# Attention maxima over every fourth query, with one transfer for each shift row

## The chip, the cores and the metric

The kernel runs on one core of a Trainium2 chip. The metric is the device time of one execution in microseconds (us). A core has TensorE (PE in the profile, with its weight loads listed apart as PEld), VectorE (DVE), ScalarE (ACT), GpSimd (POOL) and SyncE (SP), whose queue issues most of the transfers.

## The reference

A transformer block for one sequence of 2048 tokens with 512 channels: a modulated layer norm, attention with 32 heads of 16 channels, a second modulated layer norm, a token mixer with shifts, and an MLP with 1792 hidden channels. What matters here is the attention:

```python
qkv = (x @ wqkv).reshape(B, S, 3, H, Dh).transpose(2, 0, 3, 1, 4)
q, k, v = qkv[0], qkv[1], qkv[2]
scores = jnp.einsum("bhqd,bhkd->bhqk", q, k) * (Dh ** -0.5)
p = _softmax(scores, axis=-1)
o = jnp.einsum("bhqk,bhkd->bhqd", p, v)
...
x = x + ga * _A_ref(h, A_wqkv, A_wo)
h = _layernorm(x, axis=-1) * (1 + cb) + sb
x = x + gb * _B_ref(h, B_w1, B_w2, B_w3, B_w4)
```

The softmax needs the largest score of each query before it takes exponentials, so that these stay in range.

## The kernel before

The work goes in three parts: the projections to queries, keys and values (with the layer norm), the attention, and the tail with the output projection, the mixer and the MLP. The first part runs on into the first quarter of the attention.

**Units.** The attention is cut into 64 units: four chunks of 512 queries (`ci`), and in each 16 pairs of heads (`pr`). The two heads of a pair, j = 0 and 1, lie on partitions 0 to 63 and 64 to 127 of the tiles `qtl` (queries, 512 columns) and `kst` (keys, 2048 columns), which exist three times each and are loaded by `load_unit`. A head takes 48 of its 64 partitions for a query or key in three parts (a high part twice and a low part, which together give more digits). Partitions 62 and 63 of a half are the shift rows: the key tile has ones there, so what stands in the query tile's rows 62 and 63 is added to every score of that query.

**Maxima first, scores later.** A unit's keys are passed over twice. `max_part` multiplies 128 queries (the weights of the product, taken from rows 0 to 61 of `qtl`) with 512 keys, and VectorE's `reduce_max` (line 989) reduces the product over its keys into one column of `mxs`. Four groups of queries (`g`), four stretches of keys (`c`) and two heads make 32 such products for each unit. In the code before, group `g` takes every second query of half `g // 2` of the chunk, starting at `g % 2` (line 986), so that its 128 words lie two words apart in a row of `qtl`.

When a unit's last maxima are there, `max_fin` reduces over the four stretches, turns the maxima into shifts, and splits them into two parts in `nm` (partition p, part i, column 4 j + g). `shift_rows` then writes them into the rows 62 and 63 of the query tile. Since a maximum stands on a partition and must go to a column, each transfer reads all 128 partitions and writes one row; before, there are two such transfers for a row (`h`), each over half of the 512 columns, with two neighbouring columns of `nm` for each partition. There are four rows (j and i), thus eight transfers for a unit, all on SP's queue. They are issued through `sch.dma`.

`score_part` later multiplies 128 keys with the 512 queries, shift rows included; ScalarE (line 1005) turns the product into exponentials written in a form whose high and low 16 bits are used apart. GpSimd or ScalarE makes the low part ready (`p_low`, line 1058), and `pv_part` multiplies both with the values (lines 1080 and 1083).

**Order of the work.** All orders are written out when the program is built. Time runs in steps `s`, one for each 128 keys of a unit, and half-steps for the two heads. Three half-steps make a block (`GRP`). `row_pair` puts a score product of one head and a maxima product of the other side by side, on the two halves of TensorE's rows. The maxima run 24 steps ahead of the scores (`LEAD`), so a unit's shift is asked for some nine steps before its first score. Products of both kinds take turns in seven PSUM banks (`NSM`). The planner `Sched` keeps an estimated clock for each engine and for SP's queue: `sch.dma` books

```python
self.T["S"] = max(self.T["S"], self.T["P"]) + max(n / DBW, 475.0)
```

for each transfer (in ns), and the times it returns decide where later stores, releases and pieces of the projections are put in the order.

Of the kernel before, what the change touches and what calls it, by code (L numbers as in the profile page):

```python
# [8 lines left out]
F32 = mybir.dt.float32  # L9
# [318 lines left out]
def kernel(ctx, tc, A_x, A_wqkv, A_wo, B_w1, B_w2, B_w3, B_w4, c, w_mod, out):  # L328
    nc = tc.nc
    te, act, dve, pool, dma = nc.tensor, nc.scalar, nc.vector, nc.gpsimd, nc.sync  # L330
# [21 lines left out]
    def mark(key):  # L352
        return None, 0, lambda: done.add(key)
# [64 lines left out]
    sch = Sched()  # L418
# [535 lines left out]
    qst, vst, mxs = {}, {}, {}  # L954
# [18 lines left out]
    def bank(nm):  # L973
        x = sm.take()
        return x, ap_.tile([P, CH], F32, name=nm, tag=f"s{x}", bufs=1)

    def max_part(m, j):

        u, i = divmod(m, 16)
        c, g = divmod(i, 4)  # L980
        if u not in mxs:
            mxs[u] = at.tile([P, 2, 4, NC], F32, name="mx", tag="mx", bufs=2)
        x, b = bank("mb")
        ready, sm.t[x] = sm.t[x], LATE
        r = slice(64 * j, 64 * j + 62)
        lhs = qst[u][r, (g // 2) * 256:(g // 2 + 1) * 256].rearrange("p (n l) -> p l n", l=2)[:, g % 2]

        def after(e):
            end = sch.crit("D", 605, e + PX, lambda: dve.reduce_max(mxs[u][:, j, g, c:c + 1], b, axis=AX.X))  # L989
            sm.t[x] = end + XP["D"]  # L990
            if (c, g, j) == (NC - 1, 3, 0):
                max_fin(u)
        return ready, lambda: te.matmul(b, lhs, kst[u % 3][r, c * CH:(c + 1) * CH], start=True, stop=True), after  # L993
# [17 lines left out]
    def row_pair(s, j):  # L1011

        parts = []
        if 0 <= s < NS:
            parts.append((j, score_part(s, j)))
        if s + LEAD < NS:
            parts.append((1 - j, max_part(s + LEAD, 1 - j)))
        parts = [x for _, x in sorted(parts, key=lambda x: x[0])]

        def mms():  # L1020
            for _, mm, _ in parts:
                mm()
        e = sch.put("P", CROW, max(x[0] for x in parts), mms)
        return [partial(x[2], e) for x in parts]

    def max_fin(u):
        mf = at.tile([P, 8], F32, name="mf", tag="mf", bufs=2)
        nm = at.tile([P, 2, 8], F32R, name="nm", tag="nm", bufs=2)
        mx = mxs.pop(u)

        def shift_rows():
            for j in range(2):
                for i in range(2):
                    r = 64 * j + 62 + i
                    for h in range(2):
                        sch.dma(dma.dma_start,
                                qst[u][r:r + 1, h * 256:(h + 1) * 256].bitcast(F32).rearrange("o (p l) -> o p l", l=2),
                                nm[:, i, 4 * j + 2 * h:4 * j + 2 * h + 2].bitcast(F32))
        sch.chain(("D", 85, lambda: dve.reduce_max(mf.rearrange("p (j g) -> p j g", j=2), mx, axis=AX.X)),
                  ("A", 100, lambda: act.activation(mf, mf, AF.Copy, scale=-1.0, bias=PEXP)),  # L1040
                  ("A", 100, lambda: act.activation(nm[:, 0], mf, AF.Copy)),
                  ("G", 250, lambda: pool.tensor_tensor(nm[:, 1], mf, nm[:, 0], op=OP.subtract)),
                  (None, 0, shift_rows), mark(("shift", u)), prio=0, ready=sch.T["D"])
# [554 lines left out]
    for k, blk in enumerate(blocks + [[]] * (LAG + CPER)):  # L1598
# [22 lines left out]
        n = 0  # L1621
# [105 lines left out]
```

## Time and profile before

| What | Value |
|---|---|
| Median of 3 runs | 2027.61 us (2023.54 to 2027.86) |
| Profiled execution, its own time | 2030.02 us |
| Its span, first to last instruction | 2028.2 us |
| Mean granted TensorE clock | 0.987 |
| Maxima products, and transfers of shift rows | 2048, and 512 |

Lines of the profile name a line of the code, an engine, an operation, and the tiles as output <- inputs: `mb` is a maxima product, `sc` a score product, `pt` the exponentials, `pv` the sum over values, `mx` the maxima, `nm` the shifts. In groups, the numbers behind the count are the busy time in us, the mean of one in ns, and the engine's idle time before them in us with what ended it. A matmul's record holds its passage through the array as well, so that several overlap; weight loads (PEld) run beside matmuls. `SPq` is SP's queue.

### The profile page before, as it was taken

To read this page: it belongs to the slowest core of one execution; us is meant where nothing else is said; L and a number is where in the kernel's file an instruction comes from. 1 tells how busy PE (TensorE), PEld (TensorE's weight loads), DVE (VectorE), ACT (ScalarE), POOL (GpSimd) and SP (SyncE) were. 2 spreads that over 40 slices of the span, in tenths; PEclk is the share of its full clock that TensorE was granted. 3 is DMA by queue.
4 is the path that set the end of the run, shared out by engine and by line. 5 is a ranking of instruction groups with operands and counts; after the bars stand their busy time and mean duration, and the time that the engine had idled before them with its cause. 6 is when DMAs were issued, how large, how long until landed. Compare 5 with 4: busy or idle time off the path is not lost.

```text
span 2028.2 us, 41674 instructions
## 1 busy us (share of the span) xinstructions
PE 1941.1 (96%) x14456; PEld 1168.8 (58%) x14456; DVE 1658.8 (82%) x2979; ACT 1511.4 (75%) x3085; POOL 1569.9 (77%) x1488
## 2 busy tenths in 40 slices
PE   8999999999999999999999999999998889999999
PEld 5755554554444444444444444444447778898998
DVE  6398788879999999999999999999965786556443
ACT  6438887768999989999999999999984554344443
POOL 6349998879999999999999999999994554335222
PEclk9989999999999999999999999999999899999999
DMA  8877666544443435353434343454414677553541
GB/s 302 233 203 183 158 190 165 135 126 118 81 97 81 97 72 106 72 107 72 107 72 98 80 102 76 95 162 93 90 38 146 228 261 274 218 201 122 200 154 68
DMA packets 185508, 278.01 MB, mean 137 GB/s; under 512 B 117104, under 2 KB 127856, under 8 KB 169008
## 3 DMA queue, kind: packets, MB, share of 16 engines
q1 hardware_dynamic: 181792, 267.20, 49.0%
q10 hardware_dynamic: 2304, 4.20, 0.6%
q0 software_dynamic: 1200, 3.93, 0.5%
q8 instruction: 115, 1.88, 0.4%
q14 instruction: 97, 0.79, 0.1%
HBM read 211.81 MB, written 62.91 MB: 135 GB/s over the span
## 4 chain that ended last, share of the span: by engine, by line
PE 61%; DVE 16%; ACT 10%; issue 6%; POOL 4%; DMA 3%; SPq 1%; ACTq 0%; POOLq 0%; DVEq 0%
PE mb L993 13%; DVE mx L989 11%; PE pv L1083 9%; PE sc L1009 8%; ACT pt L1005 7%; PE w L360 6%; PE w L356 6%; PE w L358 6%; PE pv L1080 4%; PE ot L1110 3%; POOL pt L1058 2%; PE xT L1244 1%; DMA wr<-Ws 1%; DMA wst<-in_A_wqkv_dram 1%; SPq L132 1%
## 5 line engine op out<-in xcount | busy, mean ns | idle before, releaser
L989 DVE TENSOR_REDUCE mx<-mb 128x1 f32<-128x512 f32 x2048 | 1250.1, 680 | 74.5 <-PE mb L993 68.6
L1058 POOL TENSOR_SCALAR pt<-pt 128x1024 f16<-128x1024 uint16 x953 | 1248.1, 1365 | 78.7 <-ACT pt L1005 75.7
L1005 ACT ACTIVATE pt<-sc 128x512 int32<-128x512 f32 x2048 | 1061.3, 615 | 125.6 <-PE mb L993 98.0
L993 PE MATMUL mb<-kst,qtl 62*128 62x512 f32 x2048 | 782.7, 462 | 19.9 <-ACT pt L1005 9.9
L1009 PE MATMUL sc<-qtl,kst 64*128 64x512 f32 x2048 | 739.7, 449 | 5.0 <-DVE mx L989 2.5
L993 PEld LDWEIGHTS mb<-kst,qtl 62*128 62x128 f32 x2048 | 360.1, 193 | 232.3 <-ACT pt L1005 159.9
L1009 PEld LDWEIGHTS sc<-qtl,kst 64*128 64x128 f32 x2048 | 337.0, 186 | 186.8 <-DVE mx L989 119.3
L1083 PE MATMUL pv<-pt,vst 128*32 128x512 f16 x4096 | 385.3, 397 | 20.5 <-ACT ac L1100 20.5
L1456 POOL TENSOR_TENSOR g<-sq,g 128x256 fp32r<-128x256 f32 (+1 forms) x124 | 97.2, 787 | 200.6 <-ACT g L1455 187.2
L1080 PE MATMUL pv<-pt,vst 128*32 128x512 f16 (+1 forms) x2048 | 220.8, 389 | 2.5 <-POOL pt L1058 2.4
L1083 PEld LDWEIGHTS <-vst 128*32 128x32 bf16 x4096 | 91.8, 93 | 227.7 <-issue 209.2
L358 PE MATMUL w<-A,wr 128*128 128x256 f32 (+1 forms) x520 | 156.1, 300 | 0.3 <-DVE A L346 0.3
L356 PE MATMUL w<-A,wr 128*128 128x256 f32 (+1 forms) x520 | 155.9, 300 | 0.2 <-ACT A L350 0.2
L360 PE MATMUL w<-A,wr 128*128 128x256 f32 (+1 forms) x520 | 155.8, 300 | 0.0
L1452 ACT ACTIVATE sq<-w 128x256 f32<-128x256 f32 (+1 forms) x130 | 52.3, 402 | 136.0 <-PE w L360 127.2
L356 PE MATMUL w<-wr,g 128*128 128x512 f32 x270 | 106.9, 396 | 2.9 <-DMA wr<-Ws 2.9
L360 PE MATMUL w<-wr,g 128*128 128x512 f32 x270 | 106.5, 394 | 0.9 <-POOL g L1456 0.9
L358 PE MATMUL w<-wr,g 128*128 128x512 f32 x270 | 106.1, 393 | 0.0
L1434 DVE SCALAR_TENSOR_TENSOR sq<-sq,w 128x256 f32<-128x256 f32 (+1 forms) x130 | 58.3, 449 | 57.7 <-ACT sq L1454 57.5
L356 PEld LDWEIGHTS w<-A,wr 128*128 128x128 f32 x520 | 101.7, 196 | 1.6 <-ACT A L350 0.5
L358 PEld LDWEIGHTS w<-A,wr 128*128 128x128 f32 x520 | 101.5, 195 | 1.5 <-DVE A L346 0.5
L360 PEld LDWEIGHTS w<-A,wr 128*128 128x128 f32 x520 | 101.3, 195 | 0.5 <-issue 0.5
(156 smaller groups left out, 2128.5 us busy)
## 6 DMA issues: line engine op xcount, KB each, us to landing
wr<-Ws SPq DMA_DIRECT2D x66, 1024.0 KB, 5.5
vst<-Vs SPq DMA_DIRECT2D x64, 768.0 KB, 5.6
kst<-Ks SPq DMA_DIRECT2D x126, 384.0 KB, 6.2
Ws<-wr SPq DMA_DIRECT2D x14, 1024.0 KB, 6.2
qtl<-Qs SPq DMA_DIRECT2D x128, 96.0 KB, 4.3
Vs<-vt SPq DMA_DIRECT2D x32, 384.0 KB, 4.2
Ks<-qk SPq DMA_DIRECT2D x16, 512.0 KB, 4.2
Qs<-qk SPq DMA_DIRECT2D x16, 512.0 KB, 3.0
```

What stands on the lines that cost most here:

```text
L356: te.matmul(o, lh, rh, start=first, stop=False)
L358: te.matmul(o, lh, rl, start=False, stop=False)
L360: te.matmul(o, ll, rh, start=False, stop=last)
L989: end = sch.crit("D", 605, e + PX, lambda: dve.reduce_max(mxs[u][:, j, g, c:c + 1], b, axis=AX.X))
L993: return ready, lambda: te.matmul(b, lhs, kst[u % 3][r, c * CH:(c + 1) * CH], start=True, stop=True), after
L1005: ea = sch.crit("A", 480, e + PX, lambda: act.activation(pt[s][:, j], b, AF.Exp))
L1009: return ready, lambda: te.matmul(b, kst[u % 3][r, kt * P:(kt + 1) * P], qst[u][r], start=True, stop=True), after
L1058: e_low[s] = XP["G"] + sch.crit("G", 1345, ready, lambda: pool.tensor_scalar(o, i, 0.5, 1.0, op0=OP.mult, op1=OP.mult))
L1080: te.matmul(acc[r:r + n, :], v[:, kt + i, c:c + n].bitcast(F16), pt[s + i].bitcast(F16)[:, j, 0::2], start=False, stop=kt == NKT - 2, skip ...
L1083: te.matmul(acc[r:r + 32, :], v[:, kt, r:r + 32], pt[s].bitcast(F16)[:, j, 1::2], start=kt == 0, stop=False, skip_group_check=True)
L1110: te.matmul(b[:, t * n:(t + 1) * n], ac[:, t * P:(t + 1) * P], smat.rearrange("p j d -> p (j d)"), start=True, stop=True)
L1456: ("G", cG(n), lambda: pool.tensor_tensor(lo, sq, hi, op=OP.subtract)), (None, 0, end), bank=b)
```

## The change

A group of a maxima product takes every fourth query of the whole chunk, starting at `g`, instead of every second of a half. With that the four maxima on a partition belong to four neighbouring queries, and a shift row is written by one transfer with four columns of `nm` instead of two transfers with two. The number of maxima products, of reductions and of all other instructions stays as it was; the transfers of shift rows go from eight to four for each unit.

```diff
@@ -983,7 +983,7 @@
         r = slice(64 * j, 64 * j + 62)
-        lhs = qst[u][r, (g // 2) * 256:(g // 2 + 1) * 256].rearrange("p (n l) -> p l n", l=2)[:, g % 2]
+        lhs = qst[u][r, :].rearrange("p (n l) -> p l n", l=4)[:, g]
...
@@ -1032,10 +1032,8 @@
                     r = 64 * j + 62 + i
-                    for h in range(2):
-                        sch.dma(dma.dma_start,
-                                qst[u][r:r + 1, h * 256:(h + 1) * 256].bitcast(F32).rearrange("o (p l) -> o p l", l=2),
-                                nm[:, i, 4 * j + 2 * h:4 * j + 2 * h + 2].bitcast(F32))
+                    sch.dma(dma.dma_start, qst[u][r:r + 1, :].bitcast(F32).rearrange("o (p l) -> o p l", l=4),
+                            nm[:, i, 4 * j:4 * j + 4].bitcast(F32))
```

## The prediction

> **What bounds the kernel now.** I read the time by engine first, then the windows by stage, the groups of instructions of the long stage, its waits, the chain of waits, and last the weight loads one by one.
>
> ```profile
> span 2028.2 us, 41674 instructions
> PE 1941.1 (96%) x14456; PEld 1168.8 (58%) x14456; DVE 1658.8 (82%) x2979; ACT 1511.4 (75%) x3085; POOL 1569.9 (77%) x1488
> PE 61%; DVE 16%; ACT 10%; issue 6%; POOL 4%; DMA 3%; SPq 1%; ACTq 0%; POOLq 0%; DVEq 0%
> ```
>
> ```profile
> core 0: us, PE busy (x) PEld busy (x) DVE busy (x) ACT busy (x) POOL busy (x), PEclk, DMA share, GB/s
> 130.00:500.00 370.00, 359.06 (x2768) 191.67 (x2767) 313.21 (x535) 296.78 (x613) 329.48 (x281) 0.99 0.63 162
> 500.00:1400.00 900.00, 871.24 (x7392) 412.41 (x7391) 860.71 (x1497) 829.03 (x1642) 860.38 (x734) 0.99 0.44 93
> 1530.00:2028.00 498.00, 468.94 (x2749) 419.85 (x2741) 300.92 (x599) 215.55 (x495) 202.80 (x290) 0.98 0.52 188
> ```
>
> The windows separate three stages: attention mixed with the last projections (130 to 500 us), attention alone (to 1400), and the MLP tail after about 1530. In the 900 us of attention alone no single engine is the limit: PE 871 us, DVE 861, POOL 860 and ACT 829 are busy side by side. The granted clock there is 0.99, and the DMA engines are busy 0.44 of the time. The changed lines work only in the two attention stages; the tail has neither maxima products nor shift rows.
>
> The same 900 us by groups of instructions (count, busy us, mean ns of one, idle before), and then by who waited for whom (us in total, times, longest):
>
> ```profile
> L989 DVE TENSOR_REDUCE mx<-mb 128x1 f32<-128x512 f32 x1409 | 856.7, 680 | 32.6 <-PE mb L993 29.3 <-PE sc L1009 0.7
> L993 PEld LDWEIGHTS mb<-kst,qtl 62*128 62x128 f32 x1407 | 249.6, 193 | 159.3 <-ACT pt L1005 130.4 <-DVE mx L989 16.6 <-DVE rc L1125 0.3
> L1009 PEld LDWEIGHTS sc<-qtl,kst 64*128 64x128 f32 x1407 | 232.5, 186 | 127.7 <-DVE mx L989 94.6 <-ACT pt L1005 17.1 <-issue 4.9
> PEld mb L993 <- ACT pt L1005: 130.4, 382, 0.8
> PEld sc L1009 <- DVE mx L989: 94.6, 239, 1.2
> DVE mx L989 <- PE mb L993: 29.3, 66, 0.9
> ```
>
> The reduction of the maxima (L989) alone fills 856.7 of the 900 us: 0.61 us of VectorE for each of 1409 products. PE stands before a product mostly because no PSUM bank is free: 130.4 us before maxima products until ScalarE emptied one, 94.6 us before score products until VectorE did. VectorE in turn stood 29.3 us for a maxima product. So the stage is a loop through seven shared banks (NSM in the code), and whatever lengthens the hold of a bank is felt, though not in full.
>
> **What the change touches.** Every maxima product has its own weight load, and that load is what changes: its 128 words now lie four words apart instead of two. Here are the loads of the whole run (duration ns min/median/max), and then some of them in order of time (start, duration):
>
> ```profile
> L993 PEld LDWEIGHTS mb<-kst,qtl x2048: 189/191/335, 95.5 to 1488.4; 62*128 62x128 f32 x187
> L1009 PEld LDWEIGHTS sc<-qtl,kst x2048: 182/183/332, 130.4 to 1528.9; 64*128 64x128 f32 x187
> ```
>
> ```profile
> 864.85 0.18 PEld L1009 LDWEIGHTS sc<-qtl,kst 64*128 64x128 f32 x1 [0.45 <-DVE mx L989]
> 864.86 0.30 PEld L993 LDWEIGHTS mb<-kst,qtl 62*128 62x128 f32 x2
> 864.97 0.41 PEld L1009 LDWEIGHTS sc<-qtl,kst 64*128 64x128 f32 x2
> 865.21 0.19 PEld L993 LDWEIGHTS mb<-kst,qtl 62*128 62x128 f32 x1
> ...
> 866.11 0.19 PEld L993 LDWEIGHTS mb<-kst,qtl 62*128 62x128 f32 x1 [0.24 <-ACT pt L1005]
> 866.11 0.30 PEld L1009 LDWEIGHTS sc<-qtl,kst 64*128 64x128 f32 x2
> ```
>
> A score load reads 128 neighbouring words in 183 ns. A maxima load, two words apart, takes 191 ns: 8 ns more. Two maxima loads in a row take 0.30 us together, so the second starts 0.30 - 0.19 = 0.11 us after the first; two score loads also take 0.30, so theirs is 0.30 - 0.18 = 0.12 us. Stepping by two words therefore cost no rate, only 8 ns at the end.
>
> **Cost of the wider step.** The trace holds no load that steps by four, so I bound it. From below: nothing (the load keeps its 191 ns); a gain has no reason, since the same 128 words are read. From the nearest row, by one more doubling of the step: +8 ns. From above: a step of two still gave two words for each 16 bytes at full rate, so one word for each 16 bytes costs at most twice the reading time, which adds one more 0.11 us: about 105 to 110 ns, a load of 300. The ends are far apart. The nearest row speaks for +8, but it shows a doubling that stayed inside what the reading side has in hand, and tells nothing of the reserve left. I take +50 ns, the middle, as the likeliest, and keep 0 and 105 for the range.
>
> [...]
>
> What a longer load costs is worked out in two ways. The order of one block on PE is seen in the chain of waits in order of time (start, us):
>
> ```profile
> 871.95 0.42 PE sc L1009
> 872.38 0.23 PE mb L993 x2
> 872.61 0.23 PE sc L1009 x2
> 872.83 0.03 PE mb L993
> 872.86 0.34 PE pv L1083 x4
> ```
>
> A block is three score and three maxima products in pairs on the two halves of the array. When the banks are free, its first pair takes 0.42 us, with the load in the open, and the next two 0.23 each, with their loads behind the pair before. 2048 maxima products are 683 blocks. The first maxima load of each block is in the open: 683 x 0.05 = 34 us at +50 ns and 683 x 0.105 = 72 us at +105. The later one has 0.23 - 0.19 = 0.04 us of cover; at +50 it sticks out by 0.01 (7 us), at +105 by 0.065 (44 us). If PE alone set the pace, the change would cost 34 + 7 = 41 us, or 72 + 44 = 116 us. It doesn't: PE stands before its loads for the banks, 130.4 + 94.6 us in 900, and work that starts later eats into such waits first.
>
> The second way is by the banks. In 900 us 1407 + 1407 products pass through seven banks, so one use holds a bank for 7 x 900 / 2814 = 2.24 us on average. Half the uses grow by 50 ns, the mean by 25 ns, or 1.1%. The loop runs from about 95 to 1489 us (first and last maxima load above), 1393 us: 1.1% is 16 us. At +105 it is 33 us, at +8 2.5 us. This holds while banks are the limit; where VectorE has products ready in advance, the loss is less. I take 16 us, which lies between nothing and the 41 us of PE alone.
>
> **Cost of the shift rows.** Each unit had eight transfers and has four; over 64 units that is 512 and 256, all on SP's queue.
>
> ```profile
> 876.65 5.09 SPq L132 DMA_DIRECT2D qtl<-nm  x8
> 882.05 0.31 SPq L132 DMA_DIRECT2D qtl<-Qs  x1
> ```
>
> ```profile
> L132 SPq DMA_DIRECT2D qtl<-nm x512: 468/593/1826, 121.3 to 1496.7; - x171
> who waited for it (us, times):
>   PE sc L1009: 1.4, 3
> DMA to landing us min/median/max: 1.9/2.0/5.9
> DMA packets 185508, 278.01 MB, mean 137 GB/s; under 512 B 117104, under 2 KB 127856, under 8 KB 169008
> ```
>
> An issue takes 0.59 us at the median, so a unit's shift occupies SP for 5.1 us; four would take 2.4 if each still has 128 pieces (of 16 bytes instead of 8), and 5 if an issue grew with its bytes. Behind them in the queue stand the loads of queries and keys for a later unit, which come 0.3 us after the last issue and are used by its maxima products only some sixteen half-steps later; nobody in the long stage's list of waits stands for them. For the shift itself PE stood 1.4 us in the whole run, three times. That is all that is on the path: -1.4 us at best. The 64 x 4 x 128 = 32,768 packets that vanish, of 185,508, relieve DMA engines that are not the limit. Four landings instead of eight also remove waits on PE's side, which cost nothing that a row shows. VectorE, ScalarE and GpSimd do what they did: the same maxima in the same tile, each column of it now holding other queries.
>
> One more thing moves. The kernel's planner books SP's queue for 475 ns per transfer and orders stores and releases by it; 16 units of the first stage book 4 x 475 ns less each. Orders may shift between 130 and 500 us, where PE is busy 359.06 of 370 us. I count this as nothing with about 6 us to either side, an estimate: half of the roughly 11 us that PE is idle there.
>
> **Sum.** The profiled execution took 2030.0 us, 1.8 more than its span and 2.4 above the median of 2027.6. 2030.0 + 16 - 1.4 = 2044.6 for such an execution; for the median 2.4 less, 2042 us, 0.7% slower.
>
> **Rivals.**
>
> *The load takes the step in its stride.* For it: two words apart cost 8 ns and no rate. Then +2.5 us by the banks or nothing, less 1.4: 2026 to 2029 us, no change. It also holds if the one transfer is no cheaper to issue than the two. [...] I give it 15%.
>
> *Faster, by a quicker queue.* If loads cost nothing and the planner's shorter bookings let the projections of the first stage finish sooner, the place is 130 to 500 us: the 1.4 us of waits plus up to 6 us of idle PE, 2020 to 2024 us. It decides only if the load grows by less than about 10 ns, since 25 ns already cost 8 us by the banks. Against it: nobody waits for SP there in any sum that shows. 18%.
>
> *Much slower, by a full second pass.* The load reaches 300 ns and no longer fits under the pair before it. Then 33 us by the banks, 72 by the first loads, 116 by both: 2060 to 2140 us, likeliest near 2070, because VectorE's 857 of 900 us leave PE's waits to be eaten first. 17%.
>
> *My forecast*, a load stretched by some 25 to 80 ns, has 50%: 8 to 25 us by the banks, 2034 to 2055 us.
>
> **How the numbers follow.** The three runs before lie 4.3 us apart, so about 0.2%, or 4 us, is what can be told from no change. Slower by more: the forecast with almost all of its 50, the second pass with 17, together 66%. Same: most of the 15 and a little from beside it, 14%. Faster: 18 and the edge of no change, 20%. The range runs from 2019, below the quicker queue, to 2086, past the middle of the second pass; some 7% is left out at each end. The forecast's own range is 2034 to 2055 us.
>
> **What would show it.** Right: the maxima load's median above 215 ns while the score load stays at 183; two maxima loads in a row longer than 0.30 us; VectorE's busy time in the 900 us middle below 861 with more waiting for maxima products than 29 us; the tail from 1530 us on as long as before; 256 shift transfers of about 0.6 us each and 32,768 fewer packets. Wrong: a maxima load of 190 to 200 ns, which moves the case to the first two rivals; a load near 300, which moves it to the third; a tail or a first stage that changed by more than 6 us, which would make the planner's order the cause.

## The result, and the profile after

The changed kernel takes 2059.3 us (median; 2056.4 to 2061.4), the kernel before, measured beside it, 2026.4: a ratio of 1.0161, interval 1.0147 to 1.0175. It is slower, as forecast, but by 33 us instead of some 15. The profiled execution took 2058.0 us.

The page of the changed kernel, with time by engine and the chain that ended last by engine; then its windows by stage (columns as before; the last window is placed on the tail, which starts later now):

```profile
span 2056.2 us, 41072 instructions
PE 1984.5 (97%) x14456; PEld 1309.9 (64%) x14456; DVE 1660.5 (81%) x2979; ACT 1518.9 (74%) x3087; POOL 1570.9 (76%) x1486
DMA packets 148639, 277.94 MB, mean 135 GB/s; under 512 B 80240, under 2 KB 90992, under 8 KB 132144
PE 80%; DVE 6%; ACT 5%; POOL 3%; issue 3%; DMA 2%; SPq 0%; ACTq 0%; DVEq 0%; POOLq 0%
...
500.00:1400.00 900.00, 881.54 (x7254) 501.58 (x7252) 847.80 (x1468) 817.68 (x1614) 845.68 (x720) 1.00 0.41 91
...
1560.00:2056.30 496.30, 468.58 (x2757) 419.39 (x2749) 299.70 (x600) 215.82 (x495) 203.34 (x290) 0.98 0.52 189
```

The time in which a weight load runs grew by 141 us (1168.8 to 1309.9; loads on the two halves of the rows overlap in it), and PE's share of the chain went from 61% to 80%. VectorE's total is the same within 2 us; in the 900 us of attention alone it is 13 us less busy, since less work gets done in them. The granted clock is no lower than before: 1.00 in the 900 us where it was 0.99, and 0.98 in the tail both times. The tail holds the work it held.

The loads and transfers on the query tile, over the whole run (duration ns min/median/max, first and last start):

```profile
L993 PEld LDWEIGHTS mb<-kst,qtl x2048: 304/306/336, 96.8 to 1518.9; 62*128 62x128 f32 x187
L1009 PEld LDWEIGHTS sc<-qtl,kst x2048: 182/183/327, 132.2 to 1559.4; 64*128 64x128 f32 x187
L132 SPq DMA_DIRECT2D qtl<-nm x256: 468/591/1534, 122.7 to 1524.6; - x128
```

The maxima load went from 191 to 306 ns, the score load stayed at 183. The last score product starts at 1559.4 us instead of 1528.9, 30.5 us later; from there to the end it is 496.8 us, before 499.3. The loss lies in the attention alone.

The waits in the same 900 us, after:

```profile
PEld mb L993 <- ACT pt L1005: 100.3, 333, 0.6
PEld sc L1009 <- DVE mx L989: 85.6, 201, 0.5
DVE mx L989 <- PE mb L993: 43.9, 90, 1.0
```

TensorE waits less for banks (130.4 to 100.3 us for ScalarE, 94.6 to 85.6 for VectorE), and VectorE waits more for TensorE, 43.9 us instead of 29.3. The chain in order of time (start, us) shows where it is late:

```profile
871.40 0.43 PE sc L1009
871.83 0.23 PE mb L993 x2
872.06 0.24 PE sc L1009 x2
872.30 0.15 PE mb L993
872.45 0.34 PE pv L1081 x4
```

The first three pieces of a block are as they were within 0.01 us. The last maxima product of the block holds the chain for 0.15 us, where the block quoted of before had 0.03. The products with the values, which use all rows of the array, come that much later.

### The profile page after: what moved, and what is told of

Read it like the earlier page. It is cut to its first block, busy times and chain, and to the rows that moved or that the text cites. A ratio compares the mean times of both kernels' runs of the same rounds, so it can differ in the third digit from the quotient of the medians.

```text
span 2056.2 us, 41072 instructions
## 1 busy us (share of the span) xinstructions
PE 1984.5 (97%) x14456; PEld 1309.9 (64%) x14456; DVE 1660.5 (81%) x2979; ACT 1518.9 (74%) x3087; POOL 1570.9 (76%) x1486
## 4 chain that ended last, share of the span: by engine, by line
PE 80%; DVE 6%; ACT 5%; POOL 3%; issue 3%; DMA 2%; SPq 0%; ACTq 0%; DVEq 0%; POOLq 0%
PE mb L993 20%; PE pv L1081 14%; PE sc L1009 14%; PE pv L1078 6%; PE w L360 5%; PE w L356 5%; PE w L358 5%; ACT pt L1005 3%; PE ot L1108 3%; DVE mx L989 2%; POOL pt L1056 1%; PE xT L1242 1%; DMA wr<-Ws 1%; PE q L356 1%; PE q L358 1%
## 5 line engine op out<-in xcount | busy, mean ns | idle before, releaser
L993 PE MATMUL mb<-kst,qtl 62*128 62x512 f32 x2048 | 840.8, 520 | 12.2 <-ACT pt L1005 5.5
L993 PEld LDWEIGHTS mb<-kst,qtl 62*128 62x128 f32 x2048 | 519.3, 307 | 178.6 <-ACT pt L1005 122.6
L1009 PEld LDWEIGHTS sc<-qtl,kst 64*128 64x128 f32 x2048 | 367.9, 191 | 152.0 <-DVE mx L989 106.2
```

Source lines behind the costliest of these rows:

```text
L1009: return ready, lambda: te.matmul(b, kst[u % 3][r, kt * P:(kt + 1) * P], qst[u][r], start=True, stop=True), after
```

## The experiments

Since the changed kernel alters three things, the step of the load, the number of transfers and, through the planner's bookings, the order of the instructions, the first three runs separate them. In them a transfer's booking can be scaled, so that an order is kept exactly while its transfers change (`book` scales the 475 ns). The expectations call the three explanations the load theory, the transfer theory and the order theory.

**The step alone (e1).**

```diff
-        lhs = qst[u][r, (g // 2) * 256:(g // 2 + 1) * 256].rearrange("p (n l) -> p l n", l=2)[:, g % 2]
+        lhs = qst[u][r, :].rearrange("p (n l) -> p l n", l=4)[:, g]
...
-                                qst[u][r:r + 1, h * 256:(h + 1) * 256].bitcast(F32).rearrange("o (p l) -> o p l", l=2),
+                                qst[u][r:r + 1, :].bitcast(F32).rearrange("o (p l) -> o p l", l=4)[:, :, 2 * h:2 * h + 2],
```

> The step of four alone: each row of the shift is still written by two transfers (two of the four columns each), and all engines run the instructions of the kernel before in its order. If the stretched weight load is the cause, the maxima load reads 306 ns, the score load 183, and the time is 25 to 33 us above before (ratio 1.012 to 1.016). If the planner's new order in the first stage is the cause, the load is stretched but the time stays within 6 us of before. If fewer transfers are the cause, no change.

Measured: 2058.5 us against 2027.2, ratio 1.0166 (1.0147 to 1.0186), 31.3 us. The load:

```profile
L993 PEld LDWEIGHTS mb<-kst,qtl x2048: 304/306/335, 95.5 to 1517.5; 62*128 62x128 f32 x187
```

With the order and the eight transfers of before (their pieces now lie four words apart in the row), the whole loss is there. With the next two runs, which exclude the transfers and the order, the stretched load is its cause.

**The transfers alone, on top of that step (e2).** The edit is against the changed kernel.

```diff
-                            nm[:, i, 4 * j:4 * j + 4].bitcast(F32))
+                            nm[:, i, 4 * j:4 * j + 4].bitcast(F32), book=2.0)
```

> The changed kernel with one transfer for each row, but booked in the planner as two, so that every engine keeps the order of before. Load theory: within 2 us of the run with eight transfers, at most 1.4 us below it, which is what the score products waited for the shift. Order theory: the time of before. Transfer theory: all of the loss, with the run of eight transfers at the time of before.

Measured: 2056.7 us, ratio 1.0150 (1.0132 to 1.0169): 1.8 us below e1, with intervals that overlap. Halving the transfers is worth nothing that can be told from noise.

**The order alone (e3).** The kernel before, with `book=0.5` on each of its eight transfers.

> The kernel before, with each of its eight transfers booked at half, so that every engine has the order of the changed kernel; loads and transfers are those of before. Load theory: within 6 us of before, either way. Order theory: 25 to 33 us slower than before.

Measured: 2025.2 us, ratio 0.9994 (0.9984 to 1.0004). The planner's order did not cause the loss.

**A step of three (e4).** It asks whether the load's price grows by degrees or only from a step of 16 bytes on. Shown is what replaces the lines of the changed kernel.

```diff
+        lhs = qst[u][r, 384:512] if g == 3 else qst[u][r, :384].rearrange("p (n l) -> p l n", l=3)[:, g]
...
+                    for o, n in ((0, 3), (3, 1)):
+                        sch.dma(dma.dma_start,
+                                qst[u][r:r + 1, o * P:(o + n) * P].bitcast(F32).rearrange("o (p l) -> o p l", l=n),
+                                nm[:, i, 4 * j + o:4 * j + o + n].bitcast(F32))
```

> Three of four groups of queries take every third query of the first 384, the fourth takes the last 128 side by side; two transfers for a row (of three columns and of one), order of before. [...] If only a step of 16 bytes or more is slow, the load stays at 191 ns and the time within 3 us of before. If any step above two pays in full, 306 ns and 20 to 25 us.

Measured: 2035.9 us, ratio 1.0047 (1.0032 to 1.0062), 8.7 us slower. Its loads:

```profile
L993 PEld LDWEIGHTS mb<-kst,qtl x2048: 182/248/330, 95.3 to 1497.0; 62*128 62x128 f32 x187
```

248 ns at the median, between the 191 of a step of two and the 306 of a step of four. That refutes both a threshold at 16 bytes (191 ns expected) and a full price for any step above two (306). From two words to four, each word of step adds 57 or 58 ns. A step of five or more was not run, and what in the reading of the words sets the price is not shown.

**The step of four on one head (e9).** Half of the loads stretched in full; the transfers of that head's rows are changed to match, as in e1.

```diff
+        lhs = qst[u][r, :].rearrange("p (n l) -> p l n", l=4)[:, g] if j == 0 else qst[u][r, (g // 2) * 256:(g // 2 + 1) * 256].rearrange("p (n l) -> p l n", l=2)[:, g % 2]
...
```

> The step of four for the head on partitions 0 to 63 alone, the other head keeps the step of two; eight transfers, order of before. Half of the loads read 306 ns, the mean of all about 249, which is the mean load of the run with a step of three, whose loads all but fit under the pair before. If the cost follows the mean hold of a bank, 9 to 13 us over before. If loads over 0.23 us, which stick out from behind a pair, cost more than in proportion, half of the full loss: 15 to 18 us.

Measured: 2046.7 us against 2025.0, ratio 1.0112 (1.0095 to 1.0128), 21.7 us: above both expectations, 70% of the full loss for half of the loads. With e4 it shows that the mean load is not the measure: e4 adds 0.75 x 57 - 0.25 x 8 = 41 ns in the mean and costs 8.7 us, e9 adds 57 ns and costs 21.7. A load of 248 ns still nearly fits under a pair of 0.23 us, one of 306 does not; this would explain the low price of e4, but by it e9 should have cost half of the full loss, so it is not shown. The traces of before, e1 and e9 say where the loss falls. From the first maxima product of a block to the next product that is neither score nor maxima (mean over blocks 230 to 619), e1 adds 92 ns to the blocks with maxima of heads 1, 0, 1 and 7 ns to those of heads 0, 1, 0; e9 adds 97 ns to the latter and takes 28 ns off the former. Why the second head's loads move the loss in this way and add only 10 us more is open.

**Less work for TensorE (e5, e6).** These two and the next two ask how a longer load becomes a longer time. The expectations call it the TensorE theory that the load takes TensorE's own time, and the bank theory that it lengthens the time for which a PSUM bank is held. Both runs here leave out the products of the low parts with the values; e6 has the step of four as well, as in e1.

```diff
-                        te.matmul(acc[r:r + n, :], v[:, kt + i, c:c + n].bitcast(F16), pt[s + i].bitcast(F16)[:, j, 0::2],
-                                  start=False, stop=kt == NKT - 2, skip_group_check=True)
+                        continue
...
-                                  start=kt == 0, stop=False, skip_group_check=True)
+                                  start=kt == 0, stop=kt == NKT - 1, skip_group_check=True)
```

> The kernel before without the products of the low parts with the values (2048 of TensorE's 14456 products left out, all else in the order of before); a base for the next run. It takes 512 groups of four side by side, some 0.23 us each, off TensorE: up to 118 us less if TensorE alone set the pace. VectorE's 1250 us of reductions and the tail forbid more than about 60 us. Bank theory: less than 40 us, since holds of banks hardly change. TensorE theory: 50 us or more.

> The same without low products, with the step of four and eight transfers. If a longer load competes for TensorE's time, TensorE now has room, and the step of four costs less than 20 us over the run before it. If it costs by lengthening the hold of a bank, it still costs 26 to 36 us.

Measured: e5 2000.9 us (ratio 0.9862, 0.9841 to 0.9883), 28 us below before; e6 2029.3 us (1.0009, 0.9996 to 1.0022). The step of four costs 28.4 us there, nearly as much as in e1. Base and price both lie in the bank theory's bounds. The chain that ended last, by engine, in e5 and then in e6:

```profile
PE 53%; DVE 28%; ACT 9%; issue 4%; POOL 3%; DMA 3%; SPq 1%; ACTq 0%; DVEq 0%; POOLq 0%
```

```profile
PE 72%; DVE 11%; ACT 7%; issue 4%; POOL 4%; DMA 2%; SPq 0%; ACTq 0%; POOLq 0%; DVEq 0%
```

In e5 TensorE has less of the chain than before (53% against 61%) and VectorE more (28% against 16%): there is room. The longer load uses it up, and in e6 the chain lies on TensorE again. So the number is the one that the bank theory gave, but the chain shows a path that passes from VectorE to TensorE, and that a longer hold of the banks is the way is not shown.

**More work for TensorE (e7, e8).** Each low product is issued twice, so the low part counts double; e8 has the step of four.

> The kernel before with each product of the low parts issued twice (the low part counts double in the result); a base for the next run. TensorE theory: 80 to 118 us slower, nearly all that it adds to TensorE. Bank theory: less than 60 us, since TensorE's waits for banks take up part.

> The same with twice the low products and the step of four. TensorE theory: the longer loads cost more than on the kernel before, 45 to 110 us over the run before it, since no wait is left to take them up. Bank theory: 26 to 36 us as before.

Measured: e7 2083.1 us (1.0281, 1.0261 to 1.0300), 55 us above before and thus inside the bank theory's bound; e8 2124.4 us (1.0474, 1.0456 to 1.0492). The difference is 41.3 us: above the 26 to 36 of the bank theory, below the 45 of the TensorE theory. The chain by engine, in e7 and then in e8:

```profile
PE 81%; DVE 5%; ACT 5%; issue 3%; DMA 3%; POOL 2%; SPq 1%; POOLq 0%; ACTq 0%; DVEq 0%
```

```profile
PE 84%; DVE 5%; ACT 4%; issue 2%; POOL 2%; DMA 2%; SPq 0%; POOLq 0%; DVEq 0%; ACTq 0%
```

In e7 TensorE has 81% of the chain before any load is stretched, and there the step of four costs most. The waits before the maxima loads, in the 900 us, in e5, e6, e7 and e8 in turn:

```profile
PEld mb L993 <- ACT pt L1005: 91.5, 321, 0.8
```

```profile
PEld mb L993 <- ACT pt L1005: 58.5, 241, 0.7
```

```profile
PEld mb L993 <- ACT pt L1005: 117.8, 375, 0.8
```

```profile
PEld mb L993 <- ACT pt L1005: 78.5, 240, 0.6
```

In each pair the longer load eats 33 to 39 us of the wait for ScalarE's banks. The wait of score products for VectorE's banks falls too, by 60 us from e5 to e6 (139.2 to 79.5) but only by 5 from e7 to e8 (86.0 to 81.3). So waits take up part of the longer load, less of it where TensorE has more to do, and the rest is paid. Over a spread of 82 us in the base (e5 to e7) the price moved only from 28 to 41 us: neither theory holds alone.

**A step of one (e10).** The opposite trade: the fastest load, with four transfers for a row. Shown again is what replaces the lines of the changed kernel.

```diff
+        lhs = qst[u][r, g * P:(g + 1) * P]
...
+                    for h in range(4):
+                        sch.dma(dma.dma_start, qst[u][r:r + 1, h * P:(h + 1) * P].bitcast(F32).rearrange("o (p l) -> o p l", l=1),
+                                nm[:, i, 4 * j + h:4 * j + h + 1].bitcast(F32), book=0.5)
```

> Groups of 128 neighbouring queries (step of one), four transfers for a row, 16 for a unit, booked at half so that every engine keeps the order of before. The load falls to 183 ns, 8 ns less: 1 to 3 us faster by the slope of the other runs, if nothing waits for the shift. Sixteen issues of 0.6 us take SP 9.6 us for a unit, and the last one lands 11 to 12 us after its start, about when the first score product wants it: waits for the shift of up to 2 us a unit would make it slower by up to 60 us.

Measured: 2377.8 us, ratio 1.1738 (1.1714 to 1.1762), 353 us slower, far beyond what was expected. Time by engine, loads, one wait of the whole run and the window of e10, then one unit's transfers in order of time, and last the 5.1 us after one of the waits:

```profile
span 2379.8 us, 42444 instructions
PE 2063.0 (87%) x14456; PEld 1194.3 (50%) x14456; DVE 1669.3 (70%) x2979; ACT 1524.8 (64%) x3085; POOL 1577.2 (66%) x1488
...
L993 PEld LDWEIGHTS mb<-kst,qtl x2048: 182/183/336, 95.4 to 1839.0; 62*128 62x128 f32 x187
...
PE sc L1009 <- DMA qtl<-nm: 203.3, 62, 5.1
...
500.00:1400.00 900.00, 735.81 (x5658) 328.38 (x5661) 667.77 (x1148) 642.74 (x1259) 664.51 (x564) 0.88 0.34 68
...
904.63 11.09 SPq L132 DMA_DIRECT2D qtl<-nm  x16
...
863.10:868.20 5.10, 5.10 (x27) 2.28 (x29) 1.94 (x4) 2.30 (x5) 2.22 (x2) 0.50 1.02 172
```

The load is 183 ns, as the lines say. But score products waited for the shift 62 times, about once in each of the 64 units, 203 us in all: sixteen issues take SP 11.1 us, and the last row lands 2 us later. PE is idle for 2379.8 - 2063.0 = 317 us, before for 87: 230 us more. The other 122 us are in PE's busy time, 2063.0 against 1941.1 for the same products, and the clock can account for them. The granted clock in the window is 0.88 instead of 0.99, and after the wait that ends at 863.1 us it is 0.50. The trace records 69 stretches at half clock, 421 us in all, that of before 11 and 52 us; 342 us of PE's busy time lie in them, before 44. By an estimate from these numbers, the 298 us more at half clock are 149 us lost, enough for the 122. TensorE pauses for more than 2 us 63 times, and at 52 of these pauses a stretch at half clock begins between 3 us before the end and 0.5 us after it.

None of the ten is measurably faster than the kernel before with the same computation. One transfer for a row puts the four maxima of a partition side by side in the row; a fast load wants the words of one product side by side (183 ns against 306 four words apart). The same columns cannot give both, and two transfers with two words each are the point between.

## Why the prediction was right in direction and wrong in size

**The term that was mis-sized: the load.** The prediction bounded the growth by 0 and 105 ns and took 50 as the likeliest; it is 115 ns, just above the upper bound. With it the median of 2042 fell 17 us short. The range of 2019 to 2086 held the result, but the forecast's own range of 2034 to 2055 did not. (Its 8 to 25 us lead to 2034 to 2051; the last 4 us have no term.)

Two steps led there. The first read two maxima loads in a row, 0.30 us together, as proof that the step of two runs at full rate. The same row after:

```profile
862.26 0.42 PEld L993 LDWEIGHTS mb<-kst,qtl 62*128 62x128 f32 x2
```

The loads are 115 ns longer, and the second still starts 0.42 - 0.31 = 0.11 us after the first. The two belong to the two heads, on the two halves of the array, and overlap; their distance says nothing about the rate of one. The prediction's own fence has two score loads in 0.41 us beside two in 0.30, with each at 0.18. So the upper bound, one more such distance of 0.11 us, was the author's estimate and rested on no rate that a row shows. What did speak for the step of two was the duration alone, 191 against 183 ns. The second step was to take the middle between far ends, 50 ns, for which no row spoke.

**From the load to the time.** The hold of a bank, put at 2.24 us, would grow by 57 ns or 2.6% at the measured load: 36 us over 1393. Measured with the order kept: 31.3. For TensorE alone the prediction's way gives 683 x (0.115 + 0.306 - 0.23) = 130 us. So the banks' sum came out near at this point, and near again in e6 with 28.4. But its form, a price in proportion to the mean load, is refuted: it gives 13 us for e4 and 18 for e9, measured 8.7 and 21.7. And in e6, in e8 (41.3 us) and in the changed kernel the chain lies mostly on TensorE (72, 84 and 80%), so that its own time counts. That the banks' sum is close at 115 ns is partly luck; how the load becomes time is known only as far as these runs go.

**The rivals.** The load unaffected: refuted by its 306 ns. The quicker queue: the transfers gave 1.8 us between e1 and e2, the 1.4 us of waits being all there was, and the order 0.9994; neither is clear of noise. The full second pass, at 17%, is what happened to the load; its likeliest time of 2070 was 11 us too high, and the measured 2059.3 lies just below its range of 2060 to 2140.

**The shift rows.** Four issues take 2.4 us, as worked out:

```profile
873.86 2.41 SPq L132 DMA_DIRECT2D qtl<-nm  x4
```

An issue did not grow with its bytes (591 ns against 593). The packets fell by 36,869, not 32,768: 256 transfers of 144 packets make 36,864, and e10's 512 more add 73,733, again 144 each. The 16 beyond the 128 pieces were missed, without consequence. That the shift has cover was right for eight transfers; e10 shows how little is left of it: sixteen, 6 us longer, are late in nearly every unit.

**What was to be seen.** Of the signs listed, all came but one: load above 215 ns, score load at 183, VectorE below 861 us with more than 29 us of waits, the tail as long as before, 256 transfers of about 0.6 us. The exception is the packets' count. Of the signs against the forecast one came as well, a load near 300 ns, which the prediction had assigned to the third rival.

## What to carry to other kernels

Before a layout is changed to save transfers, look at every operand that is read through it. Here 256 transfers that hardly anybody waited for were traded for 115 ns on each of 2048 weight loads. The loss was not in proportion to the loads: 57 ns on three quarters of them cost 8.7 us, 115 ns on half of them 21.7, and 115 ns on all 31.3. A load's new duration should therefore be compared with the products that run before it (0.23 us a pair here) and not only with its old one, though that this cover is what decides is not shown. To say which of several effects pays, keep the planner's order fixed while one part of the change is made.

## What the runs showed of the hardware

Two things had not been expected. The time of a weight load of 128 fp32 words depends on the step between the words: 183 ns side by side, 191 two apart, 248 three apart, 306 four apart. What sets it is not shown. And in e10, where TensorE waited for the shift in nearly every unit (62 times, 203 us in all), the granted clock in the 900 us was 0.88 instead of 0.99, with a stretch at half clock at 52 of 63 pauses, and the busy time of the same products rose by 122 us, over a third of that kernel's loss. That the waits cause the lower clock was not tried by itself.
